# Two of a head block's 32 score tiles exponentiated on VectorE, column-group value matmuls for every second key tile, and K and Q weights in one tile

## The chip, the cores and the metric

The kernel runs on one core of a Trainium2 chip. The metric is the device time of one execution in microseconds (us). PE is TensorE, ACT is ScalarE, DVE is VectorE, POOL is GpSimd, SP is SyncE; SBUF is the on-chip memory, PSUM the accumulator memory that PE writes.

## The reference

A two-layer transformer on a sequence of 2,048 rows of width 512, bf16, batch 1. Both layers use the same weights:

```python
def _A_ref(x, wqkv, wo):          # 32 heads of width 16
    q, k, v = heads of x @ wqkv
    p = softmax(einsum("bhqd,bhkd->bhqk", q, k) * 16 ** -0.5)
    return concat_heads(einsum("bhqk,bhkd->bhqd", p, v)) @ wo
def _B_ref(x, w1, w2):            # 512 -> 1792 -> 512
    return silu(x @ w1) @ w2
x = x + _A_ref(_layernorm(x), wqkv, wo)
x = x + _B_ref(_layernorm(x), w1, w2)     # and both once more
```

The exponentials are most of the elementwise work: 2 layers x 32 heads x 2048 x 2048.

## The kernel before

**Tiling.** The 2,048 queries are cut into four chunks `c` of 512, the 32 heads into eight blocks `hb` of four, the keys into 16 tiles `kt` of 128. A unit is one `(c, hb, kt)`; a layer is a loop over 512 units, `kt` fastest. In a unit, `emit_s` (L521) makes the transposed scores of four heads with four matmuls of 32 contraction rows each, one head per row group of the array. They go into two PSUM tiles `s_ps` of 128x1024 (two heads each, `pr` 0 and 1). ACT takes each through one exp into a bf16 tile `p_sb` (L586). `emit_pv` (L533) then accumulates the four heads' values in one PSUM tile `o_ps`, with a 128x128 weight for each head: `vdq` holds, for groups of `NG` = 4 key tiles, the head's 16 value columns and a column of ones in 32 of 128 columns, and zeros elsewhere, so that each head adds into its own 32 rows. POOL fills these weights (`vd_fill`, L142) one group ahead, in `NR` = 2 slots. The row of ones gives the sum of the exponentials.

**No maximum pass.** The softmax's shift is a bound instead of a maximum: row 17 of a head's 32 rows holds in K a one (`onescol`) and in Q minus the sum of |q| times `amax`, the largest |k| of the head block (`amax_bm`, L261 and L265; the product with `Bm` in step `d` of `q_piece`, L323). K and Q weights are padded from 16 to 32 columns a head (`wk_pad`, `wq_pad`).

**Order.** The instructions of PE, ACT and DVE run in the order in which the program issues them. In each unit it issues the two exps, then all four score matmuls of the *next* unit, then the values: those of the pair `pr` = 1 kept back from the unit before (`pend`) and those of this unit's `pr` = 0. At `kt` 0 only the kept ones are issued, the block's result is copied out of `o_ps` (`finish_heads`, oT, L574), and both pairs of the new block are kept.

**Buffers.** The score tiles share a pool of three (`spool`, `wide`), `p_sb` has five buffers, `o_ps` one, and everything that the pump does shares one bank (`gpool`, `narrow`).

**The pump.** All other work runs between the units, cut into steps in a queue (`Pump`): the K and Q of the next head block (`k_piece`, `amax_bm`, `q_piece` with steps a, b, d), the division of a finished block (`heads_piece`), and from chunk 1 on the previous chunk's output projection (`epilogue_pieces`: pa, pb, pc), its LayerNorm (`ln_steps`: two stats steps, `rs`, four transposes `tr`) and its feed-forward part (`ffn_pieces`: for each hidden tile steps a and b with two matmuls and d with a tanh on ACT and a DVE product; then seven steps for each output tile), and in layer 1 the next layer's LayerNorm and V (`next_pieces`). After the values of a unit the program runs `todo` steps:

```python
remaining = TT * HB - (hb * TT + kt)
total = pump.steps()
later = sum(3 for _ in range(hb + 1, HB)) + (HB - 1 - hb)
todo = -(-(total + later) // remaining) if total else 0
if left and kt < TT - 2 and pump.q:
    todo = max(todo, 1)
```

That is one step a unit nearly everywhere, and two at the start of the first layer's chunks 1 to 3. The first scores of the next head block need its QT (L328), the last step of `q_piece`.

**Around the loops.** Before the first loop LayerNorm of all chunks, K of block 0, its Q and all V (`v_two`, L292) are made; between the loops and at the end come the last chunk's projection and feed-forward part (`ffn_last`).

Of the kernel before, what the change touches and what calls it, by code (L numbers as in the profile page):

```python
# [9 lines left out]
ALU = mybir.AluOpType  # L10
# [8 lines left out]
def kernel(  # L19
# [17 lines left out]
    H = 32  # L37
# [9 lines left out]
    VS = DH + 1  # L47
    KR = 32
    NG = 4
    NR = 2  # L50
# [6 lines left out]
    vpool = ctx.enter_context(tc.tile_pool(name="vpool", bufs=2))  # L57
    qpool = ctx.enter_context(tc.tile_pool(name="qpool", bufs=3))
# [6 lines left out]
    small = ctx.enter_context(tc.tile_pool(name="small", bufs=4))  # L65
# [13 lines left out]
    wq_pad = wpool.tile([P, CT, H, 32], BF16, name="wq_pad")  # L79
    wk_pad = wpool.tile([P, CT, H, 32], BF16, name="wk_pad")  # L80
    nc.gpsimd.memset(wk_pad[:], 0.0)
    nc.gpsimd.memset(wq_pad[:], 0.0)
    cw = cpool.tile([P, 256], BF16, name="cw")
    nc.vector.memset(cw[:], 0.0)
    nc.vector.memset(cw[0:1, 128:129], 1.0)
    for j in range(4):
        nc.vector.memset(cw[0:1, 32 * j + 16 : 32 * j + 17], 1.0)
# [6 lines left out]
    onescol = cpool.tile([P, 1], FP32, name="onescol")  # L94
    mc_ps = narrow("mc_ps")
    nc.tensor.matmul(mc_ps[:, 0:1], lhsT=cw[0:1, 0:128], rhs=cw[0:1, 128:129], start=True, stop=True)
    nc.vector.tensor_copy(out=onescol[:], in_=mc_ps[:, 0:1])


# [9 lines left out]
    w2_sb = wpool.tile([P, FT, D], BF16, name="w2_sb")  # L109
    wraw = htpool.tile([P, CT, 2 * D], BF16, name="wraw", tag="ht")  # L110
    nc.scalar.dma_start(wraw[:], A_wqkv[:, 0 : 2 * D].rearrange("(ct p) f -> p ct f", p=P))
    nc.scalar.dma_start(wv_sb[:], A_wqkv[:, 2 * D : 3 * D].rearrange("(ct p) f -> p ct f", p=P))
    for ct in range(CT):
        nc.gpsimd.tensor_copy(
            out=wk_pad[:, ct, :, 0:DH],
            in_=wraw[:, ct, D : 2 * D].rearrange("p (h d) -> p h d", d=DH),
        )
        nc.gpsimd.tensor_copy(
            out=wq_pad[:, ct, :, 0:DH],
            in_=wraw[:, ct, 0:D].rearrange("p (h d) -> p h d", d=DH),  # L120
        )
# [7 lines left out]
    vs = [vpool.tile([P, TT, D], BF16, name=f"v{i}", tag="v") for i in range(2)]  # L129
    vdq = []  # L130
    for i in range(NR):
        vd = xpool.tile([P, NG, 4, P], BF16, name=f"vd{i}")
        nc.gpsimd.memset(vd[:], 0.0)
        for j in range(4):
            nc.gpsimd.memset(vd[:, :, j, 32 * j + DH : 32 * j + DH + 1], 1.0)
        vdq.append(vd)


    def vd_fill(va, hb, g, slot):
        for j in range(4):  # L140
            h = 4 * hb + j
            nc.gpsimd.tensor_copy(  # L142
                out=vdq[slot][:, :, j, 32 * j : 32 * j + DH],
                in_=va[:, NG * g : NG * (g + 1), DH * h : DH * (h + 1)],
            )
# [78 lines left out]
    def k_mm(xnT, hb, ps, cts):  # L224
        for ct in cts:
            nc.tensor.matmul(  # L226
                ps,
                lhsT=wk_pad[:, ct, 4 * hb : 4 * hb + 4, :].rearrange("p h s -> p (h s)"),
                rhs=xnT[:, ct, :],
                start=(ct == 0),  # L230
                stop=(ct == CT - 1),
            )

    def k_piece(xnTs, c, hb):
        cell = {}

        def a():
            cell["ps"] = narrow("k_ps")
            k_mm(xnTs[c], hb, cell["ps"][:, :], (0, 1))

        def b():
            k_mm(xnTs[c], hb, cell["ps"][:, :], (2, 3))
            nc.vector.tensor_scalar(  # L243
                out=KT[:, hb, c * 512 : (c + 1) * 512], in0=cell["ps"][:, :],
                scalar1=onescol[:, 0:1], scalar2=None, op0=ALU.add,
            )

        return [a, b]

    def k_two(xnTs, c, hb):  # L250
        k_ps = wide("k2_ps")
        for i in range(2):
            k_mm(xnTs[c + i], hb, k_ps[:, i, :], range(CT))
        nc.vector.tensor_scalar(
            out=KT[:, hb, c * 512 : (c + 2) * 512],
            in0=k_ps[:].rearrange("p a b -> p (a b)"),
            scalar1=onescol[:, 0:1], scalar2=None, op0=ALU.add,
        )

    def amax_bm(hb):  # L260
        nc.vector.tensor_reduce(  # L261
            out=amax[:, hb : hb + 1], in_=KT[:, hb, :], axis=AX.X, op=ALU.max,
            apply_absolute_value=True,
        )
        nc.vector.tensor_scalar_mul(out=Bm[:, hb, :], in0=E[:, :], scalar1=amax[:, hb : hb + 1])  # L265
# [8 lines left out]

    def v_piece(cellx, tt, va):
        cell = {}

        def a():
            cell["ps"] = narrow("v_ps")
            v_mm(cellx["xnT"], tt, cell["ps"][:, :], (0, 1))  # L280

        def b():
            v_mm(cellx["xnT"], tt, cell["ps"][:, :], (2, 3))
            nc.vector.tensor_copy(out=va[:, tt, :], in_=cell["ps"][:, :])

        return [a, b]

    def v_two(xnT, tt, va):
        ps = wide("v2_ps")
        for i in range(2):  # L290
            v_mm(xnT, tt + i, ps[:, i, :], range(CT))
        nc.vector.tensor_copy(out=va[:, tt : tt + 2, :], in_=ps[:, :, :])  # L292

    def q_piece(xnTs, c, hb, QTs):
        cell = {}

        def mm(cts):
            for ct in cts:
                nc.tensor.matmul(  # L299
                    cell["ps"][:, :],  # L300
                    lhsT=wq_pad[:, ct, 4 * hb : 4 * hb + 4, :].rearrange("p h s -> p (h s)"),
                    rhs=xnTs[c][:, ct, :],
                    start=(ct == 0),
                    stop=(ct == CT - 1),
                )
# [5 lines left out]
        def b():  # L311
            mm((2, 3))
            qc = qwork.tile([P, 512], BF16, name="qc", tag="qc")
            nc.vector.tensor_copy(out=qc[:], in_=cell["ps"][:, :])  # L314
# [7 lines left out]
        def d():  # L322
            nc.tensor.matmul(  # L323
                cell["ps"][:, :], lhsT=Bm[:, hb, :], rhs=cell["qu"][:], start=False, stop=True,
                skip_group_check=True,
            )
            QTs[c][hb] = qpool.tile([P, 512], BF16, name="QT", tag="qt")
            nc.vector.tensor_copy(out=QTs[c][hb][:], in_=cell["ps"][:, :])  # L328
# [84 lines left out]
    def ffn_pieces(c, emit_out):  # L413
        cell = {}
        pieces = ln_steps(c, cell)
        for ft in range(FT):
# [11 lines left out]
            def d(ft=ft, hc=hc):  # L428
                t_sb = tpool.tile([P, 2, 512], FP32, name="t_sb", tag="t")
                nc.scalar.activation(t_sb[:, 0, :], hc["ps"][:, :], ACT.Tanh, scale=0.5)  # L430
                nc.vector.scalar_tensor_tensor(  # L431
                    out=cell["hT"][:, ft, :], in0=t_sb[:, 0, :], scalar=1.0, in1=hc["ps"][:, :],
# [35 lines left out]
    def ffn_last(c, emit_out):  # L468
# [3 lines left out]
        for f2 in range(FT // 2):  # L472
# [3 lines left out]
            t_sb = tpool.tile([P, 2, 512], FP32, name="t_sb", tag="t")  # L476
# [41 lines left out]
    def emit_s(QT, hb, kt):  # L518
        tiles = [wide("s_ps") for _ in range(2)]
        for j in range(4):  # L520
            nc.tensor.matmul(  # L521
                tiles[j // 2][:, j % 2, :],
# [5 lines left out]
        return tiles  # L528

    def emit_pv(o_ps, p_sb, kt, pr):  # L530
        for jj in range(2):
            j = 2 * pr + jj
            nc.tensor.matmul(  # L533
                o_ps[:, :],
                lhsT=vdq[kt // NG % NR][:, kt % NG, j, :],
                rhs=p_sb[:, jj, :],
                start=(kt == 0 and j == 0),
                stop=(kt == TT - 1 and j == 3),
            )

# [10 lines left out]
    for L in range(2):  # L551
# [17 lines left out]
        s_now = emit_s(QTs[0][0], 0, 0)  # L569
# [6 lines left out]

        for u, (c, hb, kt) in enumerate(units):
            if kt == 0:
                if hb == 0:
                    old_attn, attn_c = (attn, c - 1)  # L580
                    new_attn = apool.tile([P, 4, D], BF16, name="attn", tag="attn")

            ps = []
            for pr in range(2):
                p_sb = ppool.tile([P, 2, 512], BF16, name="p_sb", tag="p")
                nc.scalar.activation(  # L586
                    p_sb[:].rearrange("p a b -> p (a b)"),
                    s_now[pr][:].rearrange("p a b -> p (a b)"),
                    ACT.Exp,
                    scale=float(SCALE),  # L590
                )
                ps.append(p_sb)

            if u + 1 < len(units):
                nc_, nhb, nkt = units[u + 1]
                s_now = emit_s(QTs[nc_][nhb], nhb, nkt)

            if kt == 0:
                for args in pend:
                    emit_pv(*args)  # L600
                pend = []
# [10 lines left out]
                pend = [(o_ps, ps[0], 0, 0), (o_ps, ps[1], 0, 1)]  # L612
# [11 lines left out]
            else:  # L624
                pend.append((o_ps, ps[0], kt, 0))
                for args in pend:
                    emit_pv(*args)
                pend = [(o_ps, ps[1], kt, 1)]

            if kt % NG == 0 and u > 0 and u + NG * (NR - 1) < len(units):  # L630
                _, fhb, fkt = units[u + NG * (NR - 1)]
                vd_fill(va, fhb, fkt // NG, fkt // NG % NR)
# [5 lines left out]
            if left and kt < TT - 2 and pump.q:  # L638
                todo = max(todo, 1)
            pump_some(todo)  # L640
# [5 lines left out]
        for args in pend:  # L646
            emit_pv(*args)
# [37 lines left out]
```

## Time and profile before

| | us |
|---|---|
| Median of three runs | 2176.86 |
| Lowest, highest | 2173.24, 2178.0 |
| The profiled execution's own time | 2173.48 |
| Its span, first to last instruction | 2171.7 |
| PE busy | 1934.3 (89%) |
| ACT busy | 1942.9 (89%) |
| DVE busy | 558.7 (26%) |
| POOL busy | 247.7 (11%) |
| Mean granted TensorE clock | 0.979 |

The sections to follow use the profile of one execution. Matmuls and exps overlap in the records, so that a group's busy time is not its count times the mean of one. The first loop runs from 64 to 1058 us, the second from 1147 to 2112; a `(c)` of the first layer lasts 236 us in chunk 0 and about 251 in the others, in the second layer 237 and 241.

### The profile page before, as it was taken

The page shows a single profiled execution, that of the slowest core. Times are in us where ns is not written, and L with a number is a line of the kernel's source. Part 1 is how long each engine was busy: PE and PEld are TensorE (multiplying, and loading weights), DVE is VectorE, ACT ScalarE, POOL GpSimd, SP SyncE. Part 2 cuts the span into 40 slices and gives each one's busy share as a digit, 9 for nine tenths or more (in the row PEclk, how much of TensorE's full clock was granted, in tenths as well). Part 3 has the DMA queues.
Part 4 walks back from the last instruction along what each step waited for, and adds up shares of the span by engine and source line. Part 5 has one row for each costly group of instructions (what it writes and reads, how often), then busy time and mean ns, then how long its engine had stood idle before and what let it go on. Part 6 is the DMA issues. An engine that isn't in the chain of part 4 may idle for free.

```text
span 2171.7 us, 28490 instructions
## 1 busy us (share of the span) xinstructions
PE 1934.3 (89%) x10355; PEld 712.9 (33%) x10561; DVE 558.7 (26%) x1106; ACT 1942.9 (89%) x2152; POOL 247.7 (11%) x1055
## 2 busy tenths in 40 slices
PE   3999988899898998999778999998999889998996
PEld 1333323333333333333232333333333333333332
DVE  6323222112311133112342322131113111131114
ACT  0899989999899998999418999999999999999981
POOL 3111111111011110111000111111111111111100
PEclk9999999999999999999789999999999999999997
DMA  4000000000000000000000000000000000000000
GB/s 145 1 1 1 1 1 1 1 1 1 1 1 1 1 1 1 1 1 1 1 0 1 1 1 1 1 1 1 3 8 1 1 1 8 4 1 1 6 5 10
DMA packets 8477, 11.79 MB, mean 5 GB/s; under 512 B 400, under 2 KB 7312, under 8 KB 8336
## 3 DMA queue, kind: packets, MB, share of 16 engines
q1 hardware_dynamic: 7280, 8.39, 1.1%
q8 instruction: 82, 1.34, 0.2%
q10 hardware_dynamic: 1056, 1.57, 0.2%
q14 instruction: 59, 0.48, 0.1%
HBM read 7.86 MB, written 2.10 MB: 5 GB/s over the span
## 4 chain that ended last, share of the span: by engine, by line
PE 62%; ACT 22%; issue 9%; DVE 6%; DMA 0%; ACTq 0%; DVEq 0%
PE o_ps L533 29%; ACT p_sb L586 20%; PE s_ps L521 16%; PE y_ps L400 3%; PE k_ps L226 3%; PE q_ps L299 2%; PE h_ps L393 2%; PE y_ps L372 2%; PE v_ps L270 2%; ACT t_sb L430 1%; DVE st L150 1%; PE t_ps L195 1%; DVE oT L574 1%; PE at_ps L337 1%; DVE hT L478 1%
## 5 line engine op out<-in xcount | busy, mean ns | idle before, releaser
L586 ACT ACTIVATE p_sb<-s_ps 128x1024 bf16<-128x1024 f32 x2048 | 1921.3, 1249 | 105.2 <-PE s_ps L521 105.2
L533 PE MATMUL o_ps<-p_sb,vd 128*128 128x512 bf16 x3909 | 1034.4, 383 | 19.6 <-issue 15.3
L521 PE MATMUL s_ps<-QT,KT 32*128 32x512 bf16 x4096 | 574.5, 383 | 89.9 <-ACT p_sb L586 85.7
L533 PEld LDWEIGHTS <-vd 128*128 128x128 bf16 x4096 | 317.7, 98 | 478.6 <-issue 237.4
L142 POOL COPY vd<-v 128x64 bf16<-128x64 bf16 x1024 | 231.1, 238 | 1850.8 <-PE o_ps L533 1708.8
L521 PEld LDWEIGHTS <-KT 32*128 32x128 bf16 x4096 | 175.2, 90 | 589.8 <-issue 569.1
L574 DVE CAST oT<-o_ps 128x512 bf16<-128x512 f32 x64 | 44.3, 692 | 381.1 <-PE o_ps L533 381.1
L431 DVE SCALAR_TENSOR_TENSOR hT<-t_sb,h_ps 128x512 bf16<-128x512 f32 x84 | 57.5, 685 | 301.7 <-ACT t_sb L430 301.7
L400 PE MATMUL y_ps<-w_sb,hT 128*128 128x512 bf16 x445 | 126.3, 383 | 5.4 <-DVE hT L478 4.5
L393 PE MATMUL h_ps<-xnT,w_sb 128*128 128x512 bf16 x438 | 127.0, 389 | 2.8 <-DVE xnT L196 1.0
L314 DVE CAST qc<-q_ps 128x512 bf16<-128x512 f32 x64 | 44.2, 691 | 170.3 <-PE q_ps L299 170.3
L243 DVE TENSOR_SCALAR KT<-k_ps,onescol 128x512 bf16<-128x512 f32 x56 | 42.0, 751 | 168.7 <-PE k_ps L226 168.7
L195 PE MATMUL t_ps<-ident,xn 128*128 128x128 bf16 x256 | 30.8, 263 | 57.2 <-DVE xn L183 55.4
L406 DVE SCALAR_TENSOR_TENSOR x_sb<-y_ps,x_sb 128x512 bf16<-128x512 f32 x32 | 22.1, 691 | 231.1 <-PE y_ps L400 231.1
L477 ACT ACTIVATE t_sb<-h_ps 128x1024 f32<-128x1024 f32 x14 | 14.3, 1023 | 74.9 <-PE h_ps L393 58.7
L430 ACT ACTIVATE t_sb<-h_ps 128x512 f32<-128x512 f32 x84 | 78.3, 932 | 0.0
L299 PE MATMUL q_ps<-xnT,wq_pad 128*128 128x512 bf16 x255 | 75.8, 380 | 2.5 <-DVE attn L344 2.4
L226 PE MATMUL k_ps<-xnT,wk_pad 128*128 128x512 bf16 x254 | 76.7, 392 | 0.3 <-issue 0.2
L393 PEld LDWEIGHTS <-w_sb 128*128 128x128 bf16 x448 | 44.8, 100 | 58.2 <-issue 8.6
L400 PEld LDWEIGHTS <-hT 128*128 128x128 bf16 x448 | 43.9, 99 | 60.1 <-DVE hT L478 5.6
L328 DVE CAST QT<-q_ps 128x512 bf16<-128x512 f32 x64 | 44.3, 692 | 36.6 <-PE q_ps L323 36.6
L372 PE MATMUL y_ps<-wo_sb,aT 128*128 128x512 bf16 x126 | 40.6, 423 | 7.6 <-DVE aT L367 7.3
(58 smaller groups left out, 568.2 us busy)
## 6 DMA issues: line engine op xcount, KB each, us to landing
w_sb<-in_B_w_dram SPq DMA_DIRECT2D x2, 1792.0 KB, 14.9
x_sb<-in_A_x_dram SPq DMA_DIRECT2D x4, 512.0 KB, 9.8
out_dram<-x_sb SPq DMA_DIRECT2D x16, 128.0 KB, 1.7
wraw<-in_A_wqkv_dram ACTq DMA_DIRECT2D x1, 1024.0 KB, 7.6
wv_sb<-in_A_wqkv_dram ACTq DMA_DIRECT2D x1, 512.0 KB, 10.0
wo_sb<-in_A_wo_dram SPq DMA_DIRECT2D x1, 512.0 KB, 12.4
```

Of the source, the lines that this page charges most:

```text
L142: nc.gpsimd.tensor_copy(out=vdq[slot][:, :, j, 32 * j : 32 * j + DH], in_=va[:, NG * g : NG * (g + 1), DH * h : DH * (h + 1)],)
L226: nc.tensor.matmul(ps, lhsT=wk_pad[:, ct, 4 * hb : 4 * hb + 4, :].rearrange("p h s -> p (h s)"), rhs=xnT[:, ct, :], start=(ct == 0), stop= ...
L299: nc.tensor.matmul(cell["ps"][:, :], lhsT=wq_pad[:, ct, 4 * hb : 4 * hb + 4, :].rearrange("p h s -> p (h s)"), rhs=xnTs[c][:, ct, :], star ...
L372: nc.tensor.matmul(cell["ps"][:, :], lhsT=cell["aT"][:, ct, :], rhs=wo_sb[:, ct, :], start=(ct == 0), stop=(ct == CT - 1),)
L393: nc.tensor.matmul(ps, lhsT=w1_sb[:, ct, ft * P : (ft + 1) * P], rhs=xfT[:, ct, :], start=(ct == 0), stop=(ct == CT - 1),)
L400: nc.tensor.matmul(ps, lhsT=hT[:, ft, tq * P : (tq + 1) * P], rhs=w2_sb[:, ft, :], start=(ft == 0), stop=(ft == FT - 1),)
L430: nc.scalar.activation(t_sb[:, 0, :], hc["ps"][:, :], ACT.Tanh, scale=0.5)
L431: nc.vector.scalar_tensor_tensor(out=cell["hT"][:, ft, :], in0=t_sb[:, 0, :], scalar=1.0, in1=hc["ps"][:, :], op0=ALU.add, op1=ALU.mult,)
L521: nc.tensor.matmul(tiles[j // 2][:, j % 2, :], lhsT=KT[32 * j : 32 * j + KR, hb, kt * P : (kt + 1) * P], rhs=QT[32 * j : 32 * j + KR, :], ...
L533: nc.tensor.matmul(o_ps[:, :], lhsT=vdq[kt // NG % NR][:, kt % NG, j, :], rhs=p_sb[:, jj, :], start=(kt == 0 and j == 0), stop=(kt == TT - ...
L574: nc.vector.tensor_copy(out=oT[:], in_=o_ps[:])
L586: nc.scalar.activation(p_sb[:].rearrange("p a b -> p (a b)"), s_now[pr][:].rearrange("p a b -> p (a b)"), ACT.Exp, scale=float(SCALE),)
```

## The change

- **Exps on DVE.** At key tiles 1 and 9 of each head block (`OFF`) the pair `pr` = 1 is not exponentiated by ACT. DVE makes a polynomial times a power of two in seven passes over 1,024 elements (`exp_passes`). The first, which reads the PSUM tile, is issued in the unit itself; the six others in the six units that follow, one each, ahead of that unit's pump steps. The unit itself has no pump step. Its values are issued seven units later (`late`). In K's row 18 (`lead`) these two tiles get a constant, added by a new DVE instruction in `amax_bm`.
- **Order in such a unit.** The next unit's first score pair is issued, then the kept values, then the second score pair, then the unit's own values of `pr` = 0.
- **Values in column groups.** At the odd key tiles (`COL`) a head's value matmul has a 128x32 weight, read from V directly, and writes only the head's 32 rows of `o_ps`. V is stored with 17 columns a head (16 and a one). All four heads' matmuls of such a tile are kept back and issued together in the next unit. The even tiles (`DIAG`) go on with `vdq`, now in groups of `NG` = 2.
- **Weights of K and Q** lie in one tile `wkq`, 16 columns of K and 16 of Q in turn, for both projections; a 128-wide weight starts at column 0 or 16. The 16 rows of the other kind are set to zero in the evacuation (`own`), with the ones added in the same instruction. `q_piece` adds the product with `Bm` to the stored Q on DVE instead of accumulating it in PSUM.
- **Buffers:** QT two instead of three, `small` three instead of four, a one-buffer pool `epool` for the passes.

```diff
+    NG = 2
+    COL = [1, 3, 5, 7, 9, 11, 13, 15]
+    DIAG = [kt for kt in range(TT) if kt not in COL]
+    OFF = [1, 9]
...
+        va = xpool.tile([P, TT, VW], BF16, name=f"va{i}")
+        nc.gpsimd.memset(va[:], 1.0)
...
     def amax_bm(hb):
+        if OFF:
+            ends = KT[64:P, hb, :].rearrange("p (k n) -> p k n", n=P)
+            step = OFF[1] - OFF[0]
+            ends = ends[:, OFF[0] : OFF[1] + 1 : step, :]
+            nc.vector.tensor_scalar(
+                out=ends, in0=ends, scalar1=cols[64:P, 3:4], scalar2=None, op0=ALU.add
+            )
...
+    def emit_pv(o_ps, ps, hb, kt, prs, va):
...
+                if kt in COL:
+                    h = 4 * hb + j
+                    nc.tensor.matmul(
+                        o_ps[32 * j : 32 * j + 32, :],
+                        lhsT=va[:, kt, VS * h : VS * h + 32],
+                        rhs=ps[pr][:, jj, :],
...
+    def exp_passes(s_ps, p_sb):
...
+        def split():
+            nc.vector.tensor_scalar(
+                out=z[:], in0=s_ps[:].rearrange(flat), scalar1=-127.5 / (SCALE * LOG2E),
+                scalar2=float(SCALE * LOG2E * 2**23), op0=ALU.max, op1=ALU.mult,
+            )
+        def broken():
+            nc.vector.tensor_scalar(
+                out=m[:].bitcast(I32), in0=z[:], scalar1=0x7FFFFF, scalar2=0x3F800000,
+                op0=ALU.bitwise_and, op1=ALU.bitwise_or,
+            )
...
+        return [
+            split, broken, whole,
+            lambda: horner(y[:], m[:], 0, m[:]),
+            lambda: horner(y[:], y[:], 1, m[:]),
+            lambda: horner(y[:], y[:], 2, m[:]),
+            lambda: horner(p_sb[:].rearrange(flat), y[:], 3, z[:].bitcast(FP32)),
+        ]
...
+                if pr == 1 and off:
+                    p_sb = epool.tile([P, 2, 512], BF16, name="pd_sb", tag="pd")
+                    new = exp_passes(s_now[1], p_sb)
+                    new.pop(0)()
+                    passes += new
...
+            s_now = [f() for f in (nxt_s[:1] if off else nxt_s)]
...
+                flush(u)
+                if off:
+                    s_now += [f() for f in nxt_s[1:]]
+                    emit_pv(o_ps, ps, hb, kt, (0,), va)
+                    late.append((u + 7, (o_ps, ps, hb, kt, (1,))))
+                elif kt in COL:
+                    pend.append((o_ps, ps, hb, kt, (0, 1)))
+                else:
+                    emit_pv(o_ps, ps, hb, kt, (0,), va)
+                    pend.append((o_ps, ps, hb, kt, (1,)))
+            if passes and not off:
+                passes.pop(0)()
...
+            if off:
+                todo = 0
             pump_some(todo)
```

`horner` is one `scalar_tensor_tensor` of two SBUF tiles, `(in0 + constant) * in1`; z is int32, m and y fp32.

## The prediction

> **What bounds the kernel now.** I read the engine totals, the groups with shapes kept apart, the chain of waits, the timeline of a block boundary, and the single exp records. From the totals and the groups:
>
> ```profile
> PE 1934.3 (89%) x10355; PEld 712.9 (33%) x10561; DVE 558.7 (26%) x1106; ACT 1942.9 (89%) x2152; POOL 247.7 (11%) x1055
> ```
> ```profile
> L586 ACT ACTIVATE p_sb<-s_ps 128x1024 bf16<-128x1024 f32 x2048 | 1921.3, 1249 | 105.2 <-PE s_ps L521 105.2
> ...
> L261 DVE TENSOR_REDUCE amax<-KT 128x1 f32<-128x2048 bf16 x16 | 36.6, 2286 | 0.6
> ...
> L316 DVE TENSOR_SCALAR qu<-qc 128x512 int16<-128x512 int16 x64 | 18.8, 294 | 2.2
> ...
> L478 DVE SCALAR_TENSOR_TENSOR hT<-t_sb,h_ps 128x1024 bf16<-128x1024 f32 x14 | 17.1, 1221 | 23.2 <-ACT t_sb L477 23.2
> ...
> L254 DVE TENSOR_SCALAR KT<-k_ps,onescol 128x1024 bf16<-128x1024 f32 x4 | 5.1, 1284 | 5.4 <-PE k_ps L226 3.6 <-remote 1.8
> ```
>
> PE and ACT look equally full. Which one binds shows in the chain of waits (start, length, what):
>
> ```profile
> 119.42 1.31 ACT p_sb L586
> ...
> 120.77 0.40 PE s_ps L521 x2
> ...
> 121.23 1.33 ACT p_sb L586
> ...
> 122.61 0.40 PE s_ps L521 x2
> ...
> 123.05 1.35 ACT p_sb L586
> ...
> 124.44 0.39 PE s_ps L521 x2
> ```
>
> The second score pair of the next unit issues 0.04 to 0.05 us after the unit's first exp ends (its PSUM buffer is one of three), and these ends, 120.73, 122.56 and 124.40, lie 1.835 apart: two exps of 0.917. Single records overlap, so 1249 ns is not the pace; end to end, 1,898 of 1,963 neighbouring exps are 0.917 apart, and a tanh puts in 0.490. So 2048 x 0.917 + 84 x 0.490 = 1919 of the two loops' 1959 us are ACT at its pace. It stood still for 40: 31.6 at the start of the first layer's chunks 1 to 3, where the pump does two steps a unit, 2.1 at the second layer's start, 6.6 in gaps of some 0.27 at key tile 3. PE alone is faster: after such a gap it takes 1.73 a unit (128.64 to 130.37) (timeline of a block boundary):
>
> ```profile
> 124.44 0.39 PE L521 MATMUL s_ps<-QT,KT 32*128 32x512 bf16 x2 [0.15 <-ACT p_sb L586]
> ...
> 124.76 0.61 PE L533 MATMUL o_ps<-p_sb,vd 128*128 128x512 bf16 x2
> ...
> 125.41 0.69 DVE L574 CAST oT<-o_ps 128x512 bf16<-128x512 f32 x1 [5.99 <-PE o_ps L533]
> ...
> 126.15 0.40 PE L337 MATMUL at_ps<-ident,oT 128*128 128x128 bf16 x4 [0.79 <-DVE oT L574]
> ...
> 126.48 0.40 PE L521 MATMUL s_ps<-QT,KT 32*128 32x512 bf16 x4
> ...
> 128.12 0.59 PE L226 MATMUL k_ps<-xnT,wk_pad 128*128 128x512 bf16 x2
> ...
> 128.64 0.40 PE L521 MATMUL s_ps<-QT,KT 32*128 32x512 bf16 x4
> ...
> 129.13 5.61 ACT L586 ACTIVATE p_sb<-s_ps 128x1024 bf16<-128x1024 f32 x6 [0.16 <-PE s_ps L521]
> ...
> 130.37 0.39 PE L521 MATMUL s_ps<-QT,KT 32*128 32x512 bf16 x4
> ```
>
> It gives the prices for a walk. Score block to next block: 0.32 (124.44 to 124.76). A full matmul: 0.216, in single records; two of them and back to scores: 0.53 (128.12 to 128.64), so 0.1 for the switch. Four transposes and back: 0.33 (126.15 to 126.48). Score issue to exp end, after a wait: 1.515. Call "gate" the issue of a unit's second score pair, and X the time from there to the next unit's first pair. Four exps end at 3.62 after a gate, so X may be 2.10. The gate at 126.28 (124.44 + 1.835) and the scores at 128.64 give X = 2.36, so 0.26 late; ACT's gap there is 0.268. The rule holds.
>
> **The change: ACT.** 128 exps leave: 128 x 0.917 = -117.3 us, if ACT never waits more than before.
>
> **PE.** Eight of 16 value steps become column groups. No row shows one. Bounds: four at once, like the four score matmuls that issue within 0.01 and free the array after 0.32, or one after another, 0.87. I take 0.32 (the same array split the other way, the nearest row) and keep 0.87 for the range. Eight units then cost PE nine score blocks of 0.42, four column blocks of 0.32 and a wave of 0.22, 16 full value matmuls (3.5) and some seven pump steps (3.0), 11.8 us, against ACT's 15 x 0.917 = 13.8. On average PE is no bound; at the two places it is.
>
> [...]
>
> **The stall at key tile 9.** Its second tile goes to DVE, so ACT wants the first score pair of tile 10 one exp earlier: X may be 2.10 - 0.917 = 1.18. But between, PE has behind unit 8's gate: scores 0.32, column block of tile 7 with the late pair of tile 1 (two waves, 0.53), two full matmuls and back to scores (0.54), X = 1.39 without a pump step, 1.61 with four transposes, 1.83 with two matmuls. Late: 0.21, 0.43, 0.65; none where the step is a tanh, which fills ACT. Writing out the pump's order by its rule (no step in the two units, two steps in a unit after): 44 blocks of 0.65, 3 of 0.43, 5 of 0.21, 9 of none: 31 us in 61 blocks. The three crowded blocks come apart.
>
> **The stall at key tile 1.** Unit 0 carries column matmuls 0.32 + 0.53, then oT: last column issue 0.54 + 0.38 to its end, copy 0.69, so 1.65. Then (a) where the pump holds `heads` (23 blocks): transposes at 1.70, X = 2.02, 0.84 late; unit 1 then puts tile 0's four value matmuls (0.97 with the switch) ahead of its second score pair, which issues at 3.31, its exp ending at 4.83 for 4.46: 0.37 more, 1.21 together. (b) With two matmuls in unit 0 (21 blocks): the four value matmuls wait for oT until 1.70, second pair at 2.67, exp at 4.19 for 3.62: 0.57. (c) With a tanh there, which fills ACT: 0.08 (15). Two first blocks: none. 23 x 1.21 + 21 x 0.57 + 15 x 0.08 = 41 us.
>
> **DVE.** Seven passes per tile. The first reads PSUM: 1.25 (L254 1.284, the CAST at L292 1.225). Two bitwise passes: from 0.59 (twice L316) to 1.28 (L254); L316 has some 0.17 fixed (four-element rows take 170 ns), so four times its bytes is 4 x 0.124 + 0.17 = 0.67, taken since it is the same operation. Four two-input passes: 1.22 (L478; from 0.67 to 1.28). Sum 7.5, x 128 = 960 us, DVE to some 70%. It runs in order, and a pass stands in every unit but tiles 0, 8, 1 and 9 (there the first pass), so whatever follows waits:
> - Chunk 0, six blocks a layer: `amax` (2.29 + 0.25 + about 0.3 for the new add) at tile 11, q evacuations at 13, QT at 14. DVE's ends, from the gate of unit 8: KT evacuation 5.55, pass 6.3, amax 9.2, two passes 11.7, qc and qu 12.85, pass 14.1, QT 14.85. The next block's first scores wait for QT with all of PE's queue behind them, and issue 4.17 after gate 14 (10.73) instead of 2.10: 2.07 x 12 = 25 us.
> - LayerNorm steps (two stats of 1.6 each, `rs` near 3.0 with the first apply, unit by unit with a pass of 1.25): exps 2.9 late in three blocks, 0.5 and 1.0 in three more each: 13 us.
> - `heads` and `qa` in one unit (15 blocks), qa behind the division: 0.37 each, 5.5 us.
> - The crowded blocks: the same walk gives 2.3 + 0.4 at tile 2, 0.7, 0.7, 1.0, 1.1, 0.6 at `qb`+`qd` to `pc`+`pa`, 1.4 + 0.2 round tile 9, 4.4 at `rs`+`tr`, 1.1 at `tr`+`tr`: 13.9 each, 41.7 for 31.6.
> The split of a tile frees its PSUM buffer at 1.68 after the gate, wanted at 3.3: hidden, exposed by some 0.2 only behind `heads`. The other evacuations are done 0.05 to 0.3 before the pump's next step needs their bank.
>
> [...]
>
> **The rest.** POOL: fills of 34 instead of 64 elements, as many; two 8,944-column memsets at 0.86 ns a column (L81, 4096 in 3.5 us) are 15 us for 7 removed plus 0.9, done by 30 us where v is first written at 49. Without that cover, 8 us. K and Q weights: the same matmuls; mask in the evacuations' second operand, the same row. v copies in two: +0.16 eight times under PE's 1.75 a pair. Outside the loops +1 us.
>
> **Sum.** Against the profiled execution (span 2171.7, time 2173.5): -117.3 + (31 + 41 + 41.7 + 25 + 13 + 5.5 + 2.1) - 40.3 + 1 = +2.7, so 2176; the median of the runs shown lies 3.4 above that execution: 2180.
>
> **Rivals.** (1) DVE doesn't hold anything back: if the two-input passes run like the bitwise ones (0.67), or PE has its results in time, the QT, LayerNorm and `heads` terms go and the crowded blocks stay at 31.6: -117.3 + 31 + 41 + 31.6 + 2.1 - 40.3 + 1 = -51, 2126. For: DVE is 26% busy now. Against: L478 has no such speed, and DVE is in order. (2) Slower: column matmuls don't overlap. Six one after another instead of two waves: 4 x 0.216 = 0.86 later at both places, 122 x 0.86 = +105, 2285; each 0.1 us that a column block takes beyond 0.32 costs 12 us, and from there it decides. For: no such matmul in the trace. Against: row groups do overlap. (3) The freed time is kept because PE, with its lower load, runs ahead: 2176.9 - 117.3 + 1 = 2061. Against: the gate forbids running ahead.
>
> **Numbers.** Measurement tells about 0.2% (4.4 us) from no change. The forecast, time given back: 0.50, itself 2160 to 2205. Rival 1: 0.26. Rival 2, in part or whole: 0.21. Rival 3: 0.03. The forecast's own terms reach to both sides, more upward, as a wait not listed can only add: faster 0.36, same 0.15, slower 0.49. Range: low end by rival 1 in two thirds (-35), 2142; high end by column blocks of 0.69, 2225.
>
> **What would show it.** Right: some 1,920 exps at 0.917 end to end; ACT idle before p_sb near 240 us instead of 105, in gaps of 0.2 to 1.2 at tiles 2 and 10 and 2 us at tile 0 of chunk 0; DVE near 1,500 us; column matmuls issuing four within 0.05. Chunk 0 slower than now (236 us), the second layer's chunks 1 to 3 faster (241). Wrong: column matmuls 0.2 apart; no gap at tile 10; passes far from 1.2.

## The result and the profile after

| | before | after |
|---|---|---|
| Median, us | 2175.05 (four runs) | 2251.44 (four runs) |
| Lowest to highest, us | 2173.24 to 2178.0 | 2250.19 to 2254.67 |
| Ratio to before, 95% interval | | 1.0352 [1.0334, 1.037] |
| Profiled execution: span, time | 2171.7, 2173.48 | 2248.0, 2250.19 |
| Mean granted TensorE clock | 0.979 | 0.927 |

The change costs 76 us, 3.5%. That is above the upper end of the predicted range (2225). From the page of after, the totals, the clock row, and the groups that the prediction priced (count, then busy time and mean ns of one, then idle time before them and what ended it):

```profile
PE 1904.9 (85%) x10560; PEld 590.5 (26%) x10560; DVE 1495.2 (67%) x2023; ACT 1849.0 (82%) x2024; POOL 354.5 (16%) x1048
...
PEclk9998899999899998999977989899999899999997
...
L686 ACT ACTIVATE p_sb<-s_ps 128x1024 bf16<-128x1024 f32 x1920 | 1806.0, 1086 | 263.0 <-PE s_ps L555 258.6
...
L596 DVE SCALAR_TENSOR_TENSOR y<-y,m 128x1024 f32<-128x1024 f32 x256 | 313.5, 1225 | 4.0
...
L601 DVE TENSOR_SCALAR z<-s_ps 128x1024 int32<-128x1024 f32 x128 | 155.9, 1218 | 21.6 <-PE s_ps L555 20.9
...
L607 DVE TENSOR_SCALAR m<-z 128x1024 int32<-128x1024 int32 x128 | 88.8, 694 | 4.4
```

The 1,920 exps and DVE's 1,495 us are as priced. ACT's idle time ahead of p_sb is 263 us, for 105 before and some 240 forecast. The surprise stands in the clock row: eights in both loops, where the kernel before was granted 0.99 or more (windows of 200 to 280 us). The same row of the kernel before:

```profile
PEclk9999999999999999999789999999999999999997
```

Measured as in the prediction (ends of neighbouring ACT records, less 0.917 for an exp or 0.490 for a tanh; a "gap" from here on), ACT stood still for 224.1 us in the two loops, for 40.3 before and 159.3 forecast. One block boundary of chunk 0 shows the part that was not foreseen. Timeline, start and length in us:

```profile
162.80 0.40 PE L570 MATMUL o_ps<-p_sb,va 128*32 128x512 bf16 x4
...
163.13 0.61 PE L580 MATMUL o_ps<-p_sb,vd 128*128 128x512 bf16 x2
...
165.37 0.68 DVE L359 TENSOR_TENSOR QT<-q_ps,qc 128x512 bf16<-128x512 f32 x1
...
166.11 0.46 PE L555 MATMUL s_ps<-QT,KT 32*128 32x512 bf16 x4 [1.36 <-DVE QT L359]
...
170.10 0.61 PE L370 MATMUL at_ps<-ident,oT 128*128 128x128 bf16 x4 [0.80 <-DVE oT L661]
...
171.19 1.89 PE L580 MATMUL o_ps<-p_sb,vd 128*128 128x512 bf16 x4
...
173.00 0.61 PE L555 MATMUL s_ps<-QT,KT 32*128 32x512 bf16 x2
...
173.71 3.02 ACT L686 ACTIVATE p_sb<-s_ps 128x1024 bf16<-128x1024 f32 x3 [1.34 <-PE s_ps L555]
```

At 162.80 all is as walked: four column matmuls issue together, and the next block follows 0.33 later (0.32 assumed). At 166.11 PE has waited for QT, as forecast. But behind that wait the matmuls take twice their time: the four value matmuls between 171.19 and the next score pair at 173.00 take 1.81 where the prediction put 0.97. The same stretch in windows of PE (length, busy time, instructions, granted clock):

```profile
159.47:162.89 3.42, 3.27 (x24) 1.00 0.01 2
162.89:166.30 3.41, 1.42 (x11) 1.00 0.00 0
166.30:169.71 3.41, 3.01 (x16) 0.50 0.03 7
169.71:173.13 3.42, 3.03 (x12) 0.50 0.00 0
173.13:176.54 3.41, 3.41 (x16) 0.50 0.00 0
176.54:179.95 3.41, 3.41 (x24) 1.00 0.00 0
```

PE was busy for 1.42 of 3.41 us while it waited for QT, and the next three windows were granted half the clock. The records of the granted clock hold 94.8 us at half in the execution before, 77 of them ahead of, between and behind the loops, and 329.7 us after, 249 of them within the loops.

Ahead of the first loop, 9.1 us went: the first exp starts at 73.48, before at 64.38. POOL's row, and two pieces of the chain of waits:

```profile
12.88 15.32 POOL L142 MEMSET va<- 128x8944 bf16 x2
```
```profile
13.41 7.32 DVE xn L196
...
25.62 3.77 DVE xn L196 x2
```

Elsewhere in the chain one step of the LayerNorm's xn takes 0.33 to 0.72; beside the memsets one stands for 7.32, and two together for 3.77.

### The profile page after: what moved, and what is told of

Same layout as the page of the kernel before. It is cut to its first block, busy times and chain, and to the rows that moved or that the text cites. A ratio compares the mean times of both kernels' runs of the same rounds, so it can differ in the third digit from the quotient of the medians.

```text
span 2248.0 us, 29378 instructions
## 1 busy us (share of the span) xinstructions
PE 1904.9 (85%) x10560; PEld 590.5 (26%) x10560; DVE 1495.2 (67%) x2023; ACT 1849.0 (82%) x2024; POOL 354.5 (16%) x1048
## 4 chain that ended last, share of the span: by engine, by line
PE 59%; ACT 18%; DVE 18%; issue 5%; DMA 0%; ACTq 0%; DVEq 0%
PE s_ps L555 19%; PE o_ps L580 17%; ACT p_sb L686 15%; PE o_ps L570 8%; PE y_ps L433 3%; PE h_ps L426 3%; DVE y L596 3%; PE k_ps L239 2%; ACT t_sb L463 2%; PE q_ps L327 2%; DVE st L163 2%; DVE amax L281 2%; PE y_ps L405 1%; DVE oT L661 1%; PE v_ps L290 1%
## 5 line engine op out<-in xcount | busy, mean ns | idle before, releaser
L686 ACT ACTIVATE p_sb<-s_ps 128x1024 bf16<-128x1024 f32 x1920 | 1806.0, 1086 | 263.0 <-PE s_ps L555 258.6
L555 PE MATMUL s_ps<-QT,KT 32*128 32x512 bf16 x4096 | 695.6, 400 | 140.0 <-ACT p_sb L686 113.9
L580 PE MATMUL o_ps<-p_sb,vd 128*128 128x512 bf16 x2048 | 645.6, 404 | 6.4 <-DVE oT L661 6.4
L155 POOL COPY vd<-va 128x34 bf16<-128x34 bf16 x1024 | 331.2, 337 | 1813.7 <-PE o_ps L580 1667.1
L596 DVE SCALAR_TENSOR_TENSOR y<-y,m 128x1024 f32<-128x1024 f32 x256 | 313.5, 1225 | 4.0
L570 PE MATMUL o_ps<-p_sb,va 128*32 128x512 bf16 x1792 | 215.4, 410 | 1.0 <-ACT p_sb L686 0.8
L580 PEld LDWEIGHTS <-vd 128*128 128x128 bf16 x2048 | 126.4, 99 | 272.6 <-issue 260.4
L601 DVE TENSOR_SCALAR z<-s_ps 128x1024 int32<-128x1024 f32 x128 | 155.9, 1218 | 21.6 <-PE s_ps L555 20.9
L596 DVE SCALAR_TENSOR_TENSOR pd_sb<-y,z 128x1024 bf16<-128x1024 f32 x128 | 158.4, 1237 | 3.7
L596 DVE SCALAR_TENSOR_TENSOR y<-m 128x1024 f32<-128x1024 f32 x128 | 156.0, 1219 | 0.0
L327 PE MATMUL q_ps<-xnT,wkq 128*128 128x512 bf16 x256 | 79.6, 397 | 14.6 <-DVE attn L377 14.6
```

Source lines behind the costliest of these rows:

```text
L155: nc.gpsimd.tensor_copy(out=vdq[slot][:, :, j, 32 * j : 32 * j + VS], in_=va[:, k0 : k0 + step * (NG - 1) + 1 : step, VS * h : VS * h + VS],)
L327: nc.tensor.matmul(cell["ps"][:, :], lhsT=wkq[:, ct, P * hb + DH : P * hb + DH + P], rhs=xnTs[c][:, ct, :], start=(ct == 0), stop=(ct == C ...
L555: nc.tensor.matmul(s_ps[:, jj, :], lhsT=KT[32 * j : 32 * j + KR, hb, kt * P : (kt + 1) * P], rhs=QT[32 * j : 32 * j + KR, :], start=True, ...
L570: nc.tensor.matmul(o_ps[32 * j : 32 * j + 32, :], lhsT=va[:, kt, VS * h : VS * h + 32], rhs=ps[pr][:, jj, :], start=False, stop=(kt == TT ...
L580: nc.tensor.matmul(o_ps[:, :], lhsT=vdq[d // NG % NR][:, d % NG, j, :], rhs=ps[pr][:, jj, :], start=(kt == 0 and j == 0), stop=False, skip ...
L596: nc.vector.scalar_tensor_tensor(out=out, in0=in0, scalar=POLY[k], in1=in1, op0=ALU.add, op1=ALU.mult)
```

## The experiments

Two theories were set against each other. Mine: the walk of the queues was right, and what was missed is the clock: a lighter PE that also waits at the block boundary is granted half the clock for the windows after it, just where its work is critical. The rival: the walk missed waits on DVE's passes or on PE's order, and the clock is a by-product. Ratios are to the kernel before, on the same chip.

| run | median, us (before) | ratio [95%] | clock | gaps, us |
|---|---|---|---|---|
| e1_col_only | 2211.9 (2175.83) | 1.0166 [1.0149, 1.0184] | 0.938 | 66.1 |
| e2_ones_only | 2246.35 (2175.83) | 1.0322 [1.0305, 1.034] | 0.924 | 225.8 |
| e3_warm | 2225.54 (2175.83) | 1.0228 [1.0213, 1.0244] | 0.946 | 196.0 |
| e4_one_pass | 2177.9 (2175.83) | 1.0012 [1.0002, 1.0021] | 0.956 | 152.5 |
| e5_pass_last | 2315.69 (2175.68) | 1.064 [1.062, 1.066] | 0.920 | 284.7 |
| e6_col_warm | 2186.14 (2175.68) | 1.0049 [1.0035, 1.0064] | 0.973 | 41.9 |
| e7_off5 | 2188.53 (2175.68) | 1.0058 [1.0039, 1.0077] | 0.955 | 103 |
| e8_off5_full | 2213.78 (2175.68) | 1.0174 [1.0159, 1.019] | 0.968 | 134.5 |
| e9_warm_all | 2215.0 (2174.37) | 1.0188 [1.0173, 1.0203] | 0.959 | 196.4 |
| e10_best | 2200.51 (2174.37) | 1.0115 [1.0098, 1.0132] | 0.972 | 97.3 |
| e11_warm2 | 2222.62 (2174.37) | 1.0225 [1.021, 1.0241] | 0.944 | 198.2 |
| e12_best2 | 2161.94 (2175.38) | 0.9936 [0.9922, 0.9949] | 0.976 | 60.1 |

**e1: the column groups and the weights alone.**

```diff
-    OFF = [1, 9]
+    OFF = []
```

> The changed kernel without the exps on DVE (OFF is empty); column groups, weights and buffers as changed. Clock theory (the walk was right, and what it lacked is the granted clock, which halves after PE's waits at the block boundaries, and 9 us ahead of the first loop): ACT keeps its pace of 0.917, no clock dips inside the loops but near the chunk starts, 2165 to 2180 us. Rival A (the column matmuls themselves are dear): over 2200. Rival B (DVE's queue alone makes the loss): as the clock theory.

A miss, and by what was recorded the sign of rival A, the column matmuls; e6 decides between the two. ACT does all 2,048 exps again, PE has less to do, and the kernel is 36 us slower than before: 8 ahead of the first exp, 26 in gaps, 2 elsewhere. At tile 3 alone 27 gaps add up to 30.2 us, for 14.6 before, and all of them stand next to half-clock windows. No pass stands in any queue there. At one of them the four value matmuls, 0.97 with the switch at full clock, take 1.68:

```profile
105.52 1.89 PE L580 MATMUL o_ps<-p_sb,vd 128*128 128x512 bf16 x4
107.20 1.06 PE L239 MATMUL k_ps<-xnT,wkq 128*128 128x512 bf16 x2
```

**e6: the same with PE's load put back.** After each odd unit two matmuls with a weight of zeros run into `o_ps`; they add nothing to the sum.

```diff
-    OFF = [1, 9]
+    OFF = []
...
                 elif kt in COL:
                     pend.append((o_ps, ps, hb, kt, (0, 1)))
+                    for _ in range(2):
+                        nc.tensor.matmul(o_ps[:, :], lhsT=zed[:, :], rhs=KT[:, hb, 0:512],
+                                         start=False, stop=False, skip_group_check=True)
```

> The kernel without exps on DVE and with column groups, and in every second unit two matmuls with zero weights added into o_ps (0.43 us of useless PE work where PE waits for ACT). Clock theory: PE streams in over half of every window, the dips inside the loops go, 2180 to 2195 us against 2212 without them. Rival (the column groups are slow by their own order or weight loads): 2212 or more.

As expected: 1,024 useless matmuls make the kernel 26 us faster than e1, the half clock falls from 276.3 to 122.0 us, and the gaps fall to 41.9, near the 40.3 of the kernel before. The windows of 60 to 320 us (PE, PEld, DVE, ACT, POOL busy with their instructions, then the clock), e1 first, then e6:

```profile
60.00:320.00 260.00, 227.89 (x1250) 69.82 (x1270) 75.65 (x105) 240.04 (x260) 29.18 (x136) 0.93 0.00 1
```
```profile
60.00:320.00 260.00, 241.48 (x1431) 80.19 (x1429) 78.35 (x110) 243.12 (x264) 29.54 (x138) 0.99 0.00 1
```

In the same 260 us PE makes 159 more weight loads (some records of matmuls are missing, so I count these), and ACT finishes four more instructions.

**e3 and e11: PE kept at work over the QT wait.** Six (e3) or two (e11) of those matmuls are put at the end of unit 14 in six blocks of each layer's chunk 0, where PE is about to wait for QT; everything else is the changed kernel.

```diff
                 while tgt_c < NQC and QTs[tgt_c][tgt_hb] is None:
                     pump_some(1)
+                if c == 0 and 0 < hb < HB - 1:
+                    for _ in range(6):            # e11: range(2)
+                        nc.tensor.matmul(o_ps[:, :], lhsT=zed[:, :], rhs=KT[:, hb, 0:512],
+                                         start=False, stop=False, skip_group_check=True)
```

> Six matmuls with zero weights added into o_ps while PE waits for QT at the end of blocks 1 to 6 of chunk 0, 1.3 us of useless PE work in 12 places. Clock theory: the clock no longer halves behind them, gaps at key tile 2 fall from 1.9 + 1.4 towards 0.84 + 0.37, 2220 to 2240 us. Rival B (DVE's queue): no gain, 2250 to 2256.

> As the run with six useless matmuls in PE's wait for QT, but two. Clock theory with a threshold near half of a 3.4 us window: shares of 0.28 to 0.48 in the windows round the block's end rise by 0.13 only, so some of the 12 dips stay: 2232 to 2248 us, between 2225.5 and 2251.4. Rival (the matmuls help in another way than by the clock): as with six, or none.

72 useless matmuls take 1.2 points off the ratio (1.0352 to 1.0228), about 27 us; 24 of them do the same (1.0225), against my expectation that two would be too few. "As with six" was on record as a sign that they help in another way than by the clock. The clock records say otherwise: of the 14 boundaries ahead of blocks 1 to 7 in the two chunks 0, 13 had half clock in the changed kernel, 2 have it in e3 and 3 in e11, so two matmuls were enough for the clock too. The timeline of e3 at the boundary shown above:

```profile
161.77 1.46 PE L764 MATMUL o_ps<-KT,zed 128*128 128x512 bf16 x6
...
167.24 1.04 PE L582 MATMUL o_ps<-p_sb,vd 128*128 128x512 bf16 x4
...
168.21 0.39 PE L557 MATMUL s_ps<-QT,KT 32*128 32x512 bf16 x2
```

The wait for QT is still there (gaps at tile 0: 19.7 us, 19.9 in after). But the four value matmuls now take 0.97, to the hundredth what the prediction put, and this boundary's gaps at tile 2 are 0.88 + 0.37 = 1.25 (1.21 forecast) instead of 1.95 + 1.44.

**e9: zeros everywhere.** e3's edit, e6's two matmuls in the odd units but 1 and 9, and e2's memset below.

> The changed kernel with useless matmuls (zero weights, into o_ps) behind each second unit's values and in PE's wait for QT, and with only the ones of va set. Nothing of the DVE work, of ACT's work or of the order is taken away. Clock theory: the remaining dips go but those at LayerNorm waits of 3 to 5 us, gaps at key tile 2 become 0.87 + 0.37 or 0.57 nearly everywhere, 2190 to 2205 us, close to the prediction's own sum plus what is left of the late start. Rival B: 2225 or more.

10 us above the expected range, and the loops still hold 99 us of half clock for 249; but most boundaries now show the walk without it. Outside the three crowded blocks (the starts of the first layer's chunks 1 to 3), 54 of 61 blocks fall into the prediction's three classes at tile 2, to a hundredth of each other: 21 waits of 0.59 (0.57 forecast), 13 of 0.09 (0.08), 20 of 1.24 (1.21). Of the other seven, the three behind a LayerNorm wait (3.45) and the second layer's first block (1.92) are at half clock, two stand at 0.26, and the very first block has no wait. In after, 18 of the 23 blocks with `heads` had half clock there, and stood 3.12 in the mean; the five that kept full clock stood 1.25. The zeros may have a price of their own: the crowded blocks grew from 49.9 to 58.1.

**e2: the memset.** Only the columns that need a one are set.

```diff
-        nc.gpsimd.memset(va[:], 1.0)
+        nc.gpsimd.memset(va[:, :, 0 : VS * H].rearrange("p t (h s) -> p t h s", s=VS)[:, :, :, DH:VS], 1.0)
+        nc.gpsimd.memset(va[:, :, VS * H : VW], 1.0)
```

> The memset of all of va (2 x 8944 columns) replaced by one of the ones' columns and the pad. Port theory (two DVE LayerNorm instructions stand still while POOL's memset runs, 7.3 and 3.8 us): first exp some 8 us earlier, 2240 to 2245 us. Rival (the start is late for another reason, the weights' copies or V): no change, 2251.

The first exp starts at 66.73 instead of 73.48, and the whole is 5 us shorter, 1 us above the expected range; the gaps do not move (225.8 for 224.1). Four memsets take the place of the two, the longest of them 2.42:

```profile
13.11 2.42 POOL L142 MEMSET va<- 128x512 bf16 x1
```

The longest xn in the chain is 2.25 instead of 7.32. So 6.7 of the 9.1 us at the start are the memset's, and the loops' gaps have nothing to do with it.

**e4: one pass of seven.** The first pass writes zeros into the tile's probabilities, and the six others are left out; the result lacks these exponentials.

```diff
-        return [
-            split, broken, whole,
...
+        return [split]
```

> Six of the seven passes left out: the first writes zeros as the tile's probabilities. PE's and ACT's order is kept. Clock theory: the QT, LayerNorm and crowded-block waits go, and most clock dips with them; the gaps at key tiles 2 and 10 stay at 0.6 to 1.2 and 0.65, so 2150 to 2185 us. Rival B (all of the loss is DVE's queue): gaps at tiles 2 and 10 shrink too, below 2140. Rival A (column matmuls): above 2220.

In the range expected. From its page:

```profile
PE 1835.2 (84%) x10360; PEld 587.1 (27%) x10560; DVE 733.0 (34%) x1255; ACT 1845.8 (85%) x2024; POOL 245.9 (11%) x1048
...
L660 ACT ACTIVATE p_sb<-s_ps 128x1024 bf16<-128x1024 f32 x1920 | 1804.0, 1091 | 195.0 <-PE s_ps L555 190.8
```

With DVE half as busy most of the QT waits go (5.4 us at tile 0 for 19.9), and the half clock falls from 329.7 to 193.6 us. Tile 10 doesn't move (36.7 us for 36.5): that wait is PE's order, as forecast. Even so the kernel only reaches the time of the kernel before.

**e5: the pass behind the pump's steps,** so that QT and the LayerNorm come first on DVE.

```diff
-            if passes and not off:
-                passes.pop(0)()
...
             pump_some(todo)
...
+            if passes and not off:
+                passes.pop(0)()
```

> Each unit's pass is issued behind its pump step instead of ahead of it, nothing else. Walk plus clock theory: QT no longer stands behind the pass of key tile 14, PE's wait at the block's end falls from 1.4 to some 0.3 us, so the gaps at key tile 0 of chunk 0 fall from 1.5 to 0.2 to 0.6, and where no clock dip follows those at tile 2 to 0.87 + 0.37: 2205 to 2225 us. Rival B (DVE as a whole is too slow, its order is of no matter): 2245 or more.

A clear miss. The QT gap falls from 1.5 to 0.87, but the last pass now ends after PE has come to the late values:

```profile
88.69 1.27 DVE L596 SCALAR_TENSOR_TENSOR pd_sb<-y,z 128x1024 bf16<-128x1024 f32 x1
...
90.02 0.39 PE L570 MATMUL o_ps<-pd_sb,va 128*32 128x512 bf16 x2 [0.64 <-DVE pd_sb L596]
...
91.80 4.69 ACT L686 ACTIVATE p_sb<-s_ps 128x1024 bf16<-128x1024 f32 x5 [1.36 <-PE s_ps L555]
```

PE issues what stands behind them after them, the next scores at 91.31, and ACT waits 1.36 for these. This gap, at tile 10 of the first block, is 1.47 instead of 0.65; outside the crowded blocks all gaps at tile 10 come to 91.5 us for 36.5.

**e7 and e8: one tile instead of two, away from the block boundary.** Both have e2's memset and `OFF = [5]` with no pump step in units 4 and 5; e8 makes only tile 5 a column group, so that PE has its old load.

```diff
-    OFF = [1, 9]
+    OFF = [5]
...
-    COL = [1, 3, 5, 7, 9, 11, 13, 15]      # e8 only
+    COL = [5]
```

> One tile a head block on DVE, at key tile 5, no pump step in units 4 and 5, only the ones of va set; column groups at the odd tiles. Walk: X after gate 4 is 1.18 with the column block and two value matmuls, so hardly a gap; 59 us leave ACT, the block end is free of passes. Clock theory: the dips of the column groups stay (some 26 us as in the kernel without exps on DVE), 2140 to 2175 us. Rival B: above 2200.

> As the kernel with one tile at key tile 5, but only that tile's values in column groups, so that PE keeps its load. Walk: X after gate 4 is 1.29 for 1.18 wanted, 0.11 late, 64 x (0.917 - 0.11) = 52 us saved, some 10 given back at QT and LayerNorm. Clock theory: no dips but those of the kernel before, 2120 to 2145 us, faster than the kernel before and than the one with column groups at all odd tiles. Rival (the clock is no cause, less PE work is always better): slower than that one.

Two misses. In e7 the gaps are 103 us: 26.3 at tile 13 (the LayerNorm's `rs` behind the passes), 20.6 at tile 3, 15.2 at tanhs of tile 7. In e8 the wait after the DVE tile is 0.11 to 0.17 in nearly every block (0.11 walked), but with groups of two key tiles for all 16 POOL has twice as many fills, and PE's weight loads come to wait for them (us in total, times, longest):

```profile
PEld L581 <- POOL vd L156: 35.5, 151, 0.4
```

That these waits make the loss is not shown. Both kernels keep the passes in the first layer's chunks 1 to 3, where DVE has the LayerNorm. e8 is slower than e7, which was on record as the sign of the rival (less work for PE is always better). But e8 has less half clock than e7 (144.2 us for 197.8), and its fills have doubled as well: the pair does not test the clock.

**e10 and e12: PE's work as before, passes where DVE has room.** Value matmuls, V and `NG` = 4 as in the kernel before; the DVE tile only in 37 blocks (chunk 0 of both layers, and the second layer without block 1 of chunks 1 to 3); the late values with an own weight tile `vl`. e12 moves those values to unit 14, and lays the DVE tile's probabilities into the buffer of its mantissa `m`, which makes room for the fifth `p_sb`.

```diff
+            blk = (c == 0 or L == 1) and not (L == 1 and c > 0 and hb == 1)
+            off = blk and kt in OFF
...
-    late.append((u + 7, ...))          # e10, from the change
+    late.append((u + 9, ...))          # e12
...
-    ppool = ctx.enter_context(tc.tile_pool(name="ppool", bufs=4))    # e10
+    ppool = ctx.enter_context(tc.tile_pool(name="ppool", bufs=5))    # e12
```

> A version meant to be faster than both: PE's work as before the change (all values with full weights, V as before), one tile a block on DVE at key tile 5, its late values from a weight tile of their own, only in chunk 0 of both layers and in the second layer's other blocks without LayerNorm (37 blocks), a pump step left out only in unit 4. Walk: 0.917 less 0.11 at the gate of unit 4 and up to 0.2 for the step in unit 5, so 0.6 to 0.8 a block, 22 to 30 us; some 5 given back behind QT and tanh: 2148 to 2160 us. Clock theory: no dips that the kernel before doesn't have. Rival B (DVE passes always cost more than they save): 2176 or more.

> As the run before of one DVE tile in 37 blocks (value matmuls and V as in the kernel before), with two edits: the late value pair is issued at key tile 14 instead of 12, and the pool of p_sb has five buffers again (the DVE tile's probabilities lie in the buffer of its mantissa). Theory (the queue's order): the 23.1 us of waits at tile 14 (the late values met the last pass) and the 28.0 us at tile 2 (p_sb came free late) both go; ACT's waits fall from 97 to about 46 us, near the 40 of the kernel before, and the time is that of before less 37 exponentials of 0.917 (34 us) plus 6: about 2147, at most 2160. Rival one: the waits at tile 2 belong to PE's order at the block boundary and not to the pool: they stay, tile 14 alone clears, and the time is about 2172 to 2180. Rival two: the lighter PE loses its clock: the granted clock falls below 0.96, the boundary waits grow, and the time is 2180 or more.

e10 missed. Its timeline at tile 12 of a block of chunk 0:

```profile
116.01 2.29 DVE L296 TENSOR_REDUCE amax<-KT 128x1 f32<-128x2048 bf16 x1
...
118.50 1.22 DVE L611 SCALAR_TENSOR_TENSOR pd_sb<-y,z 128x1024 bf16<-128x1024 f32 x1
119.77 0.38 PE L686 MATMUL o_ps<-pd_sb,vl 128*128 128x512 bf16 x1 [1.41 <-DVE pd_sb L611]
...
121.64 7.44 ACT L709 ACTIVATE p_sb<-s_ps 128x1024 bf16<-128x1024 f32 x8 [1.52 <-PE s_ps L570]
```

`amax` holds the last pass back, and the late values hold PE: 23.1 us at tile 14. And among ACT's waits of e10 stands one that no other kernel here has in this size:

```profile
ACT p_sb L709 <- PE o_ps L595: 21.5, 57, 2.6
```

An exp waits for the value matmuls, that is for its output buffer, one of four instead of five. In e12 this row is gone, and the gaps at tiles 2 and 14 fall from 28.0 and 23.1 us to 5.0 and 2.8. Its page:

```profile
PE 1930.4 (89%) x10354; PEld 702.9 (33%) x10560; DVE 839.1 (39%) x1387; ACT 1919.8 (89%) x2115; POOL 338.8 (16%) x1131
...
L709 ACT ACTIVATE p_sb<-s_ps 128x1024 bf16<-128x1024 f32 x1984 | 1869.6, 1179 | 118.4 <-PE s_ps L570 116.9
```

27 of its 2,011 exps stand in another row, with the bias. 2161.94 lies 2 us above the most that the theory allowed ("about 2147, at most 2160") and well below both rivals. Its sum: 37 exps of 0.917 (-33.9), gaps 60.1 for 40.3 (+19.8), the first exp 0.9 later: -13.2; between the two profiled executions it is -11.5 (2160.2 for 2171.7), so under 2 us lie in none of these terms. This version is faster than both kernels, by 0.6% [0.5%, 0.8%] against the kernel before.

## Why the prediction was wrong

Span against span, the miss is 74 us: +76.3 measured, +2.7 forecast. 65 of it lie in the loops, 9 outside. By the terms of its sum, in us:

| term | forecast | after |
|---|---|---|
| exps gone | -117.3 | -117.4 |
| tile-9 stall (gaps at tile 10) | 31 | 36.5 |
| tile-1 stall (gaps at tile 2) | 41 | 77.8 |
| crowded blocks | 41.7 | 49.9 |
| QT (gaps at tile 0) | 25 | 19.9 |
| LayerNorm (what is left at other tiles) | 13 | 22.4 |
| `heads` + `qa` (gaps at tile 4 of 15 blocks) | 5.5 | 7.8 |
| second layer's start | 2.1 | 2.1 |
| other gaps at tiles 3 and 4 | 0 | 7.6 |
| gaps of before | -40.3 | -40.2 |
| outside the loops | 1 | 10.2 |

- **Passes, column block, DVE's load: right.** 1.22 + 0.69 + 0.69 + 4 x 1.22 = 7.5 us a tile as forecast; DVE 1,495 us; a column block 0.33. Rival 2 is out: the four overlap (351 of the 353 blocks of four at full clock issue them within 0.01). Rival 1 is out too: the two-input passes take 1.22, and QT did wait.
- **Tile 9: right.** 0.65 in block after block. The 5.5 more are nine waits of 0.64 at a tanh that came in one unit with the second two of its matmuls (steps b and d); the walk had no wait at a tanh.
- **QT and LayerNorm: right in kind.** 1.5 a block instead of 2.07; 2.77 at the LayerNorm's `rs` instead of 2.9, but the smaller waits there were more and longer than listed. It is luck that QT's 5 us too many make up for tile 9's 5.5 too few.
- **`heads` + `qa`: right in kind.** The wait stands in 15 blocks, as forecast, with 0.53 instead of 0.37 each. In after, PE waits for the division (`attn`) with the scores behind it:

```profile
378.31 0.42 DVE L377 TENSOR_TENSOR attn<-at_ps,rec 128x256 bf16<-128x256 bf16 x1
...
378.79 0.60 PE L327 MATMUL q_ps<-xnT,wkq 128*128 128x512 bf16 x2 [0.81 <-DVE attn L377]
...
379.82 3.77 ACT L686 ACTIVATE p_sb<-s_ps 128x1024 bf16<-128x1024 f32 x4 [0.42 <-PE s_ps L555]
```

- **Tile 1: the step that failed.** Without half clock its classes are right to 0.03 us (e9). The step took every duration of PE from rows at full clock, and said "on average PE is no bound". The prediction named the clock nowhere as a case. But the sum that it made, 11.8 us of PE for ACT's 13.8 in eight units, with column groups that hand PE on after 0.33 where four full matmuls take 0.87, is a PE that idles; and it had put a 2 us standstill of PE, the QT wait, in front of the most critical boundary. 18 of the 23 `heads` blocks ran it at half clock: 18 x (3.12 - 1.21) = 34 us, most of the 36.8 by which the term was missed. e1 and e6 show it with ACT's work as before (276.3 us of half clock without the useless matmuls, 122.0 with them), e3 and e11 on the changed kernel (half clock at 2 and 3 of 14 boundaries for 13), each worth 26 to 28 us.
- **Other gaps at tiles 3 and 4.** No term had them. In e9 1.5 of the 7.6 us are left, behind the half clock that is left there, so they go with the clock.
- **"Done by 30 us where v is first written at 49": the second step that failed.** The memsets did end at 28.2. The step asked who needs the result, and not what stands still beside the memsets. The prediction's own price without that cover, 8 us, comes near: e2 takes back 6.7 of the 9.1 us at the first exp; the cause of the other 2.4 stays open. The two standstills, 7.32 and 3.77, lie beside memsets of 7.66 each, and without those memsets the longest xn is 2.25; why DVE stands still there was not shown.
- **Crowded blocks.** 8.2 more than forecast; half clock and late waits mix there, and no run separated them.

Of the prediction's signs, the ACT idle time (263 us for near 240), the gaps at tiles 0, 2 and 10, DVE's load, chunk 0 slower (256 us for 236) and the second layer's chunks 1 to 3 faster (238 to 240 for 242) came true, though single gaps at tile 2 reached 2.2 us where 0.2 to 1.2 was forecast. That excess was the only trace that the clock left in them; no sign asked for the clock itself.

## What to carry to other kernels

A walk of PE's queue gave its waits to a few hundredths of a microsecond here, but only at the clock that its rows were taken at: before relying on a lighter TensorE, add up how long it streams in each stretch of 3.4 us (the step of the clock's records here), above all around a wait, and keep that share up (all drops to half clock in the two executions counted below followed a share of at most 0.51; two useless matmuls at each wait gained as much here as six). Ask of each "hidden" instruction not only who waits for its result but what stands still beside it while it runs (here an xn for 7.32 us). And work moved to an idle engine paid here only where that engine's queue had room: 37 tiles in the right blocks gained 0.6%, 128 tiles, with column groups, cost 3.5%.

## What the runs showed of the hardware

- **Half clock after a half-idle window.** The records of the granted clock hold two values, 1.0 and 0.5, and all but the last record of an execution last a whole number of windows of 3.413 us. I counted, in the executions of before and after, how much of each window PE streamed (0.216 us for each 512-column matmul at full clock and 0.427 at half, the distances at which they follow each other in the rows; shorter ones in proportion, overlapping ones once). All 51 full-clock windows that were followed by half clock had a share of at most 0.51, with a median of 0.32; of the 1,092 followed by full clock, 95% had 0.53 or more, but some as little as 0.38. The clock came back after 51 half-clock windows, all with 0.68 or more, median 0.86; 72 others, median 0.54 but up to 0.86, stayed at half. So the share alone does not decide. Of the 51 windows ahead of half clock 32 had a share of 0.3 or more, and 5 were under 0.04. To come back took a larger share (0.68 at least) than to stay (0.38 was enough in one).
- **POOL's fills and DVE's passes.** A fill of `vd` takes 219 ns in the mean in e4, with one pass, and 337 ns in after, with seven; the passes themselves keep their 1.22 us. What makes the fills longer was not shown.
- **Column groups.** Four 128x32 matmuls issue within 0.01 of each other and the next full matmul follows after 0.33 us; their four weight loads (0.10 together in the timeline, at 162.80) lie within that time.
